# Seven quarter products for the second expert matmul, with paced loads and turns at PSUM banks in the schedule

## The chip, the cores and the metric

The kernel runs on one core of a Trainium2 chip. The metric is the time of one execution in device microseconds. Before the change the median was 1172.03 us of three runs (1170.56 to 1175.1).

Words used throughout: PE is the matmul engine (PEld its weight load), DVE the vector engine, ACT the scalar engine, POOL the GpSimd engine, SP the engine that issues some of the DMA. SBUF is the on-chip memory, PSUM the memory, in banks, that matmuls write into. The granted PE clock is the share of PE's full clock that the chip let it have. To "turn" is to transpose. A "group" is 512 tokens; there are nine groups and eight experts. A "pair" is two attention heads of one batch; there are 32 pairs.

## The reference

```python
def phi(x):                       # attention with exp features
    proj = einsum('bhsd,df->bhsf', x, w_phi)
    proj = proj - max(abs(proj), axis=-1)
    return concatenate([exp(proj), exp(-proj)])
q_p, k_p = phi(q), phi(k)
kv = einsum('bhsf,bhsd->bhfd', k_p, v);  z = sum(k_p, axis=2)
x  = einsum(q_p, kv) / (einsum(q_p, z) + 1e-6)          # -> 4608 x 512
P  = 8 rounds of row and column normalising of exp(x @ w_gate)
for e in range(8):
    h = maximum(x @ w1[e], 0)     # 4608 x 1024
    out += P[:, e] * (h @ w2[e])  # 4608 x 512
```

Batch 8, 8 heads, 576 positions of 64, 128 features; tokens 4608, model width 512, expert width 1024.

## The kernel before

The kernel does not write its instructions in program order. It records every operation with a modelled duration, then a list scheduler (`Plan`) puts them in order of modelled start time, engine by engine. The engines follow that fixed order; each waits, on the chip, for what its next instruction really depends on. So the modelled times decide only the order.

```python
    def start(self, o, free):            # modelled start of an operation
        t = max(free, o.ready)           # engine free, dependencies done
        ...                              # a buffer of the ring is free
        return t
```

Expert 0 is interleaved with attention, one unit per pair with a lag of six pairs, since attention loads DVE and ACT more than PE. Its weights are loaded whole, after the first pair:

```python
    def stage_b(j):
        ...
            if j == 0:
                W[0] = load_w(0, [(xbs[j], 0)])     # two DMAs of 2 MB (f32)
    def stage_a(i):
        ...
            load_qk(b + 1, 2 * pr, 4, t)            # next batch, no gate
            load_v(b + 1, 2 * pr, 4, t)
            if b + 1 >= 1:
                turn_qk(t)                          # DMA transpose for every batch but the first
```

After attention and the routing (P), experts 1 to 7 run, group after group. For each group 32 matmuls of 128x512 make the hidden layer (`up`, ACT does the relu into `hT`), and 32 more the output (`down`), each output tile of 128 tokens being scaled by P and added to `acc` by DVE:

```python
            for t0 in range(0, 4, 1):
                py = down(w2, hT, range(t0, t0 + 1), ["P"])    # 8 matmuls of 128x512
                ...
                    if e == 1:
                        pool(850, ... tensor_scalar(acc *= P[:, :, 0]))
                    dve(560, ... scalar_tensor_tensor(acc += P * py))
```

The softmax here doesn't subtract the row's maximum and nothing guards it: scores larger than these inputs give would overflow.

## Time and profile before

| | before |
|---|---|
| median time | 1172.03 us |
| PE busy | 1120.7 us, 96% |
| DVE, ACT, POOL busy | 35%, 44%, 18% |
| first up-matmul of expert 1 | 295.9 us |
| from there to the end | 874.7 us |
| period of one group of experts 1 to 7 | 13.81 us |

First, the busy time of each engine in four stretches of the kernel before (microseconds from the start of the span, engine by engine with the count of instructions; then the granted PE clock, the share of the DMA engines' time that packets took, which can exceed 1, and GB/s).

```profile
core 0: us, PE busy (x) PEld busy (x) DVE busy (x) ACT busy (x) POOL busy (x), PEclk, DMA share, GB/s
0.00:100.00 100.00, 71.29 (x665) 45.06 (x672) 66.42 (x157) 65.69 (x167) 62.67 (x119) 0.85 1.13 153
100.00:200.00 100.00, 91.99 (x983) 58.28 (x997) 85.89 (x208) 88.07 (x228) 57.85 (x118) 1.00 0.74 123
200.00:300.00 100.00, 95.36 (x784) 53.35 (x796) 70.31 (x168) 58.44 (x136) 40.21 (x62) 0.98 0.23 43
600.00:700.00 100.00, 99.53 (x456) 45.35 (x464) 21.79 (x29) 34.19 (x58) 1.64 (x2) 1.00 0.14 22
```

In the expert stage (last line) PE has hardly a gap and the rest is mostly idle: there only less PE work helps. In the first 250 us PE idles at times; between 100 and 200 us DVE and ACT are 86 and 88% busy. In the first 100 us the granted clock is 0.85; the lowest part is this:

```profile
30.00:50.00 20.00, 12.78 (x120) 8.77 (x119) 10.88 (x29) 6.10 (x19) 6.69 (x17) 0.50 1.40 157
```

The PE timeline of the kernel before, in one group of the expert stage (start, length, operation, count):

```profile
703.39 0.59 PE L353 MATMUL P_7735<-w_6754,hT 128*128 128x512 bf16 x2
703.83 0.81 PE L353 MATMUL P_7739<-xT,w_6625 128*128 128x512 bf16 x3
...
710.73 1.46 PE L353 MATMUL P_7735<-w_6754,hT 128*128 128x512 bf16 x6
712.03 1.89 PE L353 MATMUL P_7794<-w_6754,hT 128*128 128x512 bf16 x8
```

The up-matmuls start at 703.83 and, a period later, again at 717.64: 13.81 us for 64 matmuls, 0.216 us each.

The chain of waits of the kernel before, in its first 60 us, has one piece that stands out, and the copies that end each pair (DVE, xT) show what it did:

```profile
25.62 20.93 DMA w_442<-in_moe_w_dram
46.60 0.61 PE P_738 L353
```

```profile
L581 DVE COPY xT<-P_676 x1: 414/414/414, 43.2 to 43.2; 128x512 bf16<-128x512 bf16 x1
L581 DVE COPY xT<-P_1087 x1: 424/424/424, 74.0 to 74.0; 128x512 bf16<-128x512 bf16 x1
L581 DVE COPY xT<-P_1205 x1: 411/411/411, 80.9 to 80.9; 128x512 bf16<-128x512 bf16 x1
```

PE stood in front of expert 0's first matmul until w1 had landed at 46.6 us (its wait there was 2.5 us by the view of waits); the scores of the fifth pair were behind it in PE's order and started at 60.0 us. Pair 4 was done at 43.2 us, pair 5 at 74.0. The last pair was done at 250.6 us.

In the score step DVE (largest absolute value) and ACT (two exponentials) read the same PSUM bank. The timeline of ACT and DVE there (in brackets: idle time before, and what ended it):

```profile
149.34 0.61 ACT L349 ACTIVATE k_2627<-P_2611 128x512 bf16<-128x512 f32 x1
149.99 0.69 DVE L345 TENSOR_REDUCE m<-P_2611 128x4 f32<-128x512 f32 x1 [0.29 <-ACT k_2627 L349]
150.71 0.60 ACT L349 ACTIVATE k_2638<-P_2611 128x512 bf16<-128x512 f32 x1 [0.76 <-DVE m L345]
```

All three read bank P_2611. DVE waits until ACT's first read is over, and ACT's second read waits 0.76 us for DVE. Nothing but the shared bank connects them.

### The profile page before, as it was taken

The page shows a single profiled execution, that of the slowest core. Times are in us where ns is not written, and L with a number is a line of the kernel's source. Part 1 is how long each engine was busy: PE and PEld are TensorE (multiplying, and loading weights), DVE is VectorE, ACT ScalarE, POOL GpSimd, SP SyncE. Part 2 cuts the span into 40 slices and gives each one's busy share as a digit, 9 for nine tenths or more (in the row PEclk, how much of TensorE's full clock was granted, in tenths as well). Part 3 has the DMA queues.
Part 4 walks back from the last instruction along what each step waited for, and adds up shares of the span by engine and source line. Part 5 has one row for each costly group of instructions (what it writes and reads, how often), then busy time and mean ns, then how long its engine had stood idle before and what let it go on. Part 6 is the DMA issues. An engine that isn't in the chain of part 4 may idle for free.

```text
span 1170.6 us, 15841 instructions
## 1 busy us (share of the span) xinstructions
PE 1120.7 (96%) x6361; PEld 549.3 (47%) x6476; DVE 411.9 (35%) x783; ACT 510.9 (44%) x1028; POOL 208.9 (18%) x333
## 2 busy tenths in 40 slices
PE   5777999999999999999999999999999999999998
PEld 3444656654444444444444444444444444444443
DVE  6478888875122222222222222222222222222222
ACT  6488988843433333333333333333333333333331
POOL 9365555513960000000000000000000000000000
PEclk8699999999999999999999999999999999999999
DMA  9988776600040040003100220022000400002112
GB/s 175 156 136 132 131 116 113 127 1 1 1 71 2 3 70 1 1 1 46 28 1 1 36 36 1 1 37 36 1 1 4 69 1 1 1 1 73 72 72 108
DMA packets 87242, 54.45 MB, mean 47 GB/s; under 512 B 47616, under 2 KB 80512, under 8 KB 87168
## 3 DMA queue, kind: packets, MB, share of 16 engines
q0 software_dynamic: 38448, 26.23, 16.7%
q1 hardware_dynamic: 48720, 27.20, 10.2%
q8 instruction: 50, 0.82, 0.3%
q14 instruction: 24, 0.20, 0.1%
HBM read 61.95 MB, written 9.44 MB: 61 GB/s over the span
## 4 chain that ended last, share of the span: by engine, by line
PE 84%; ACT 6%; DVE 4%; DMA 3%; issue 2%; POOL 1%; ACTq 0%; DVEq 0%; POOLq 0%
DMA w_442<-in_moe_w_dram 2%; DVE m L345 1%; DVE xb L559 1%; DMA qkT<-qk 1%; DMA qk_r<-in_q_dram 1%; ACT hT L631 0%; POOL qk L293 0%; DVE rec L557 0%; PE P_4657 L353 0%; POOL qk_r L336 0%; DVE xb_r L564 0%; DVE m_r L345 0%; PE P_4707 L353 0%; PE P_10337 L353 0%; PE P_9770 L353 0%
## 5 line engine op out<-in xcount | busy, mean ns | idle before, releaser
L353 PEld LDWEIGHTS <-hT 128*128 128x128 bf16 x2304 | 225.1, 98 | 264.8 <-issue 2.2
L353 PEld LDWEIGHTS <-w_3748 128*128 128x128 bf16 x288 | 28.2, 98 | 34.0
L353 PEld LDWEIGHTS <-w_5820 128*128 128x128 bf16 x288 | 28.2, 98 | 34.0
L353 PEld LDWEIGHTS <-w_8235 128*128 128x128 bf16 x288 | 28.2, 98 | 34.0
L353 PEld LDWEIGHTS <-w_9040 128*128 128x128 bf16 x288 | 28.2, 98 | 34.0
L353 PEld LDWEIGHTS <-w_5377 128*128 128x128 bf16 x288 | 28.2, 98 | 33.9
L353 PEld LDWEIGHTS <-w_7430 128*128 128x128 bf16 x288 | 28.2, 98 | 34.0
L353 PEld LDWEIGHTS <-w_6625 128*128 128x128 bf16 x288 | 28.2, 98 | 34.0
L353 PEld LDWEIGHTS <-w_442 128*128 128x128 bf16 x288 | 26.6, 100 | 28.6 <-issue 6.5
L353 PEld LDWEIGHTS <-qkT 128*128 128x128 bf16 x256 | 24.8, 101 | 19.7 <-issue 3.6
L282 POOL DMA_DIRECT2D w_6625<-in_moe_w_dram x1 | 0.8, 754 | 103.1 <-PE P_6616 L353 103.1
L282 POOL DMA_DIRECT2D w_8235<-in_moe_w_dram x1 | 0.8, 752 | 103.1 <-PE P_8226 L353 103.1
L282 POOL DMA_DIRECT2D w_9040<-in_moe_w_dram x1 | 0.8, 752 | 103.1 <-PE P_9031 L353 103.1
L282 POOL DMA_DIRECT2D w_7430<-in_moe_w_dram x1 | 0.8, 752 | 103.1 <-PE P_7421 L353 103.1
L293 POOL DMA_DIRECT2D qk<-in_k_dram x17 | 13.6, 801 | 10.3 <-DMA qkT<-qk 5.6
L293 POOL DMA_DIRECT2D qk<-in_q_dram x17 | 13.0, 762 | 0.0
L850 POOL TENSOR_SCALAR acc_82<-acc_82,P 128x512 f32<-128x512 f32 x4 | 6.2, 1555 | 37.3 <-DVE P L814 37.3
L282 POOL DMA_DIRECT2D w_5820<-in_moe_w_dram x1 | 0.8, 752 | 67.3 <-PE P_5811 L353 67.3
L578 PEld LDWEIGHTS <-xb 128*128 128x128 bf16 x128 | 8.7, 101 | 5.7 <-issue 3.8
L353 PEld LDWEIGHTS <-wphi_72 128*128 128x128 bf16 x72 | 6.7, 102 | 4.9 <-issue 4.0
L349 ACT ACTIVATE r<-m 128x8 f32<-128x8 f32 x32 | 7.7, 239 | 0.0
L854 DVE SCALAR_TENSOR_TENSOR acc_82<-P_5169,P,acc_82 128x512 f32<-128x512 f32 x1 | 0.8, 751 | 16.7 <-PE P_5169 L353 16.7
(3557 smaller groups left out, 2621.8 us busy)
## 6 DMA issues: line engine op xcount, KB each, us to landing
v_m<-in_v_dram SPq DMA_DIRECT2D x15, 512.0 KB, 4.7
qk<-in_k_dram POOLq DMA_DIRECT2D x15, 256.0 KB, 5.2
qk<-in_q_dram POOLq DMA_DIRECT2D x15, 256.0 KB, 5.8
w_442<-in_moe_w_dram POOLq DMA_DIRECT2D x1, 1024.0 KB, 20.9
w_458<-in_moe_w_dram POOLq DMA_DIRECT2D x1, 1024.0 KB, 27.1
w_3748<-in_moe_w_dram POOLq DMA_DIRECT2D x1, 1024.0 KB, 9.4
w_3770<-in_moe_w_dram POOLq DMA_DIRECT2D x1, 1024.0 KB, 15.1
w_5377<-in_moe_w_dram POOLq DMA_DIRECT2D x1, 1024.0 KB, 8.3
```

What stands on the lines that cost most here:

```text
L282: dma("POOL", 2 << 20, 280, lambda: nc.gpsimd.dma_start(out=w1(), in_=moe_w1[e].rearrange("(c p) f -> p c f", p=128)), r, [w1])
L293: dma("POOL", nh << 17, 230, lambda x=x, src=src: nc.gpsimd.dma_start(out=t["qk"]()[:, x, o:o + nh], in_=src[b, hh:hh + nh, 0:SM].rearrang ...
L345: dve(el, lambda: nc.vector.tensor_reduce(out=dst(), in_=src(), axis=AX.X, op=ALU.max, apply_absolute_value=True), r, w)
L349: act(el, lambda: nc.scalar.activation(out=dst(), in_=src(), func=ACT.Exp, bias=0.0, scale=scale), r, w)
L353: nc.tensor.matmul(out_, lhsT=lhsT, rhs=rhs, start=start, stop=stop)
L559: dve(256, lambda: nc.vector.tensor_tensor(out=xb()[:, :, h * 64:h * 64 + 64], in0=num()[:, 0:4, 0:D], in1=rec()[:, 0:4, None].to_broadcas ...
L578: pe(128, lambda j=j: nc.tensor.transpose(bf(pxt)[:, j * 128:j * 128 + 128], xb()[:, j, :], ident), [(xb, 0), (xb, 1), "ident"], [pxt])
L850: pool(850, lambda g=g, ts=ts: nc.gpsimd.tensor_scalar(out=acc[g][:, ts, :], in0=acc[g][:, ts, :], scalar1=P[:, 4 * g + ts, 0:1], scalar2= ...
L854: dve(560, lambda g=g, ts=ts, i=i, py=py, e=e: nc.vector.scalar_tensor_tensor(out=acc[g][:, ts, :], in0=py()[:, 512 * i:512 * i + 512], sc ...
```

## The change

The intent: cut the second expert matmul of experts 1 to 7 into quarters (two halves of the tokens and of the contraction, two halves of the contraction and of the output) and compute it with seven products of quarters in place of eight, with Strassen's scheme in Winograd's form. A product is 8 matmuls of 128x256, so 56 of them replace 32 of 128x512, an eighth less PE work in the second matmul. The sums of quarters of w2 (T) are made once per expert on POOL, those of h (S) once per group, two on DVE and two on POOL. Three PSUM banks serve a group; the bank x holds four products one after the other, each added to what is there, and DVE reads it between. In the same change come a new start (expert 0's weights in eight pieces, loads gated on the progress of the pairs, the second batch turned by PE instead of by DMA) and a rule in the scheduler: an operation on a PSUM bank starts, in the model, only after another engine's last use of that bank has ended ("turns"). The scaling of `acc` by expert 0's P moves from POOL to ACT.

The diff, cut to its core (cuts marked with ...):

```diff
@@ def start(self, o, free)
+            elif b.last is not None and b.last.eng != o.eng:
+                t = max(t, b.last.end)
@@ def schedule(self)
             for b in o.bufs:
+                if b.ring.psum:
+                    b.last = o
...
@@ def rest_a / def pair_a
-        if b < 1:
+        if b < 2:                      # turn by PE
@@ def stage_a(i)
+        gt = [("max", 0, i - 1)] if i >= 1 else []
...
-            load_qk(b + 1, 2 * pr, 4, t)
-            load_v(b + 1, 2 * pr, 4, t)
-            if b + 1 >= 1:
+            load_qk(b + 1, 2 * pr, 4, t, gt)
+            load_v(b + 1, 2 * pr, 4, t, gt)
+            if b + 1 >= 2:
                 turn_qk(t)
...
+        n = i - 2
+        if 0 <= n < 8 * 1 and n % 1 == 0:
...
+                    load_w0(1 * (n // 1) + y, [("max", 0, i - 1)] if i >= 1 else [])
@@ def stage_b(j)
-            if j == 0:
-                W[0] = load_w(0, [(xbs[j], 0)])
@@
+    def sums_w(w2):                    # four POOL subtractions of 128x1024 per expert
...
+    def down7(e, g, hT, w2, T):
...
+        add(pool, 2, lambda: a(0, 0), lambda: a(1, 0), ALU.subtract, hk[0])
+        add(dve, 0, lambda: a(1, 0), lambda: a(1, 1), ALU.add, hk[0] + hk[1])
+        add(dve, 1, lambda: S[0](), lambda: a(0, 0), ALU.subtract, [S[0]] + hk[0])
+        add(pool, 3, lambda: a(0, 1), lambda: S[1](), ALU.subtract, [S[1]] + hk[1])
...
+        product(y, lambda: a(0, 1), lambda: b(1, 0), hk[1], True)
+        read(y, 0, 0)                                  # read: two DVE operations of 128x256
+        product(x, lambda: a(0, 0), lambda: b(0, 0), hk[0], True)
...                                                     # ACT copies x to U, POOL adds U to acc
+        product(z, lambda: S[0](), lambda: T()[:, 0], [S[0], (T, 0)], True)
+        read(z, 1, 1)
+        product(x, lambda: S[1](), lambda: T()[:, 1], [S[1], (T, 1)], False)
+        read(x, 0, 1)
+        product(x, lambda: S[2](), lambda: T()[:, 2], [S[2], (T, 2)], False)
+        read(x, 1, 1)
+        product(z, lambda: S[3](), lambda: b(1, 1), [S[3]], False)
+        read(z, 0, 1)
+        product(x, lambda: a(1, 1), lambda: T()[:, 3], hk[1] + [(T, 3)], False)
+        read(x, 1, 0)
```

More of the change, by code (lines that the diff above doesn't have):

```diff
@@ L21, in __init__ @@
         self.ring, self.t, self.slot, self.left, self.end = ring, None, None, 0, 0.0
+        self.last = None
     def __call__(self):
@@ L29, with __init__ @@
 class Ring:
-    def __init__(self, pool, shape, dtype, tag, bufs):
+    def __init__(self, pool, shape, dtype, tag, bufs, psum=False):
+        self.psum = psum
         self.free = [(0.0, i) for i in range(bufs)]
@@ L201 @@
     P = const.tile([128, NT, E], FP32, name="P")
-    vrd = [[const.tile([128, NP, 2, D1], BF16, name=f"vrd{i}{x}") for x in range(2)]
-           for i in range(2)]
     NA = 5
@@ L209 @@
     a_in = tc.alloc_tile_pool(name="a_in", bufs=1)
+    vrd = [[a_in.tile([128, NP, 2, D1], BF16, name=f"vrd{i}{x}") for x in range(2)]
+           for i in range(2)]
     a_t = tc.alloc_tile_pool(name="a_t", bufs=1)
@@ L236, in ring @@
         R[tag] = Ring((lambda: p) if not isinstance(p, str) else (lambda: late[p]),
-                      shape, dtype, tag, bufs)
+                      shape, dtype, tag, bufs, p is ps)
     ring(wp, [128, 4, FF], BF16, "w1", 2)
@@ L263 @@
         ring(a_s, [128, 8], FP32, f"em{x}", 2)
+    ring("s_p", [128, 4, 4, 256], BF16, "T", 2)
+    ring("s_p", [128, 4, 256], BF16, "S", 8)
+    ring("s_p", [128, 2, 256], FP32, "U", 2)
     ring("s_p", [128, NT, E], FP32, "u", 1)
@@ L282, in load_w, with load_w0, load_qk @@
         dma("POOL", 2 << 20, 280, lambda: nc.gpsimd.dma_start(
-            out=w1(), in_=moe_w1[e].rearrange("(c p) f -> p c f", p=128)), r, [w1])
+            out=w1(), in_=moe_w1[e].rearrange("(c p) f -> p c f", p=128)),
+            r, [(w1, i) for i in range(4)])
         dma("POOL", 2 << 20, 280, lambda: nc.gpsimd.dma_start(
-            out=w2(), in_=moe_w2[e].rearrange("(c p) f -> p c f", p=128)), r, [w2])
+            out=w2(), in_=moe_w2[e].rearrange("(c p) f -> p c f", p=128)),
+            r, [(w2, i) for i in range(4)])
         return w1, w2
-    def load_qk(b, hh, nh, t):
+    def load_w0(i, r):
+        w1, w2 = W[0]
+        n = i % 4
+        if i < 4:
+            dma("POOL", 1 << 19, 250, lambda: nc.gpsimd.dma_start(
+                out=w1()[:, :, n * 256:(n + 1) * 256],
+                in_=moe_w1[0].rearrange("(c p) f -> p c f", p=128)
+                [:, :, n * 256:(n + 1) * 256]), r, [(w1, n)])
+        else:
+            dma("POOL", 1 << 19, 280, lambda: nc.gpsimd.dma_start(
+                out=w2()[:, 2 * n:2 * n + 2, :],
+                in_=moe_w2[0].rearrange("(c p) f -> p c f", p=128)
+                [:, 2 * n:2 * n + 2]), r, [(w2, n)])
+    def load_qk(b, hh, nh, t, r=()):
         o = hh % 4
@@ L295, in load_qk, with load_v @@
                 in_=src[b, hh:hh + nh, 0:SM].rearrange("h (p j) d -> p h (j d)", j=NJ)),
-                w=[(t["qk"], x, i) for i in keys])
-    def load_v(b, hh, nh, t):
+                r, [(t["qk"], x, i) for i in keys])
+    def load_v(b, hh, nh, t, r=()):
         o = hh % 4
@@ L303, in load_v @@
             in_=v[b, hh:hh + nh, 0:SM].rearrange("h (p j) d -> p h (j d)", j=NJ)),
-            w=[(t["v"], i) for i in keys])
+            r, [(t["v"], i) for i in keys])
     def turn_qk(t, pr=None):
@@ L323, in new_half, with load_rests @@
         return {"qk": new("qk"), "T": new("qkT"), "v": new("v_m")}
-    def load_rests(b0, nb):
+    def load_rests(b0, nb, r=()):
         t = {"qk": new("qk_r"), "v": new("v_r"), "b0": b0}
@@ L336, in load_rests @@
                     nc.gpsimd.dma_start(out=t["qk"]()[rows, 0:NP * nb, x, :], in_=part(src)),
-                    w=[(t["qk"], h, x)])
+                    r, [(t["qk"], h, x)])
             dma("SP", nb << 16, 150, lambda rows=rows, part=part: nc.sync.dma_start(
-                out=t["v"]()[rows, 0:NP * nb], in_=part(v)), w=[(t["v"], h)])
+                out=t["v"]()[rows, 0:NP * nb], in_=part(v)), r, [(t["v"], h)])
         for b in range(b0, b0 + nb):
@@ L421, in pair_a @@
         s = {}
-        if b < 1:
+        if b < 2:
             for x in (1, 0):
@@ L457, in scores @@
                       lambda pp=pp: pp().rearrange("p (a b) -> p a b", a=4 * n),
-                      [pp], [(m, x, c0)])
+                      [pp], [(m, x, c0), ("max", x, NP * b + pr)])
                 if x == 1:
@@ L629, in up @@
                         xT[:, dc, g * 512:(g + 1) * 512], dc == 0, dc == NP - 1),
-                        xkeys(g, dc) + [w1, *r], [ph, *w], [hT])
+                        xkeys(g, dc) + [(w1, (f0 + i) // 2), *r], [ph, *w], [hT])
             act(512 * n, lambda f0=f0, ph=ph: nc.scalar.activation(
@@ L642, in down @@
                     w2()[:, fc, :], fc == 0, fc == 7),
-                    [(hT, f) for f in (range(8) if fc == 0 else (fc,))] + [w2, *r], [(py, i)])
+                    [(hT, f) for f in (range(8) if fc == 0 else (fc,))]
+                    + [(w2, f) for f in range(4)] + [*r], [(py, i)])
         return py
@@ L681 @@
     load_v(0, 0, 2, halves[0, 0])
-    if 1 == 0:
+    if 2 == 0:
         turn_qk(halves[0, 0], 0)
@@ L692 @@
     load_v(0, 2, 2, halves[0, 0])
-    if 1 == 0:
+    if 2 == 0:
         turn_qk(halves[0, 0], 1)
@@ L696 @@
     load_v(0, 4, 4, halves[0, 1])
-    if 1 == 0:
+    if 2 == 0:
         turn_qk(halves[0, 1])
@@ L708 @@
     rs, st = {}, {}
+    W[0] = (new("w1"), new("w2"))
     def expert0(i):
@@ L728, in stage_a @@
             t = halves[b + 1, pr // 2]
-            load_qk(b + 1, 2 * pr, 4, t)
-            load_v(b + 1, 2 * pr, 4, t)
-            if b + 1 >= 1:
+            load_qk(b + 1, 2 * pr, 4, t, gt)
+            load_v(b + 1, 2 * pr, 4, t, gt)
+            if b + 1 >= 2:
                 turn_qk(t)
-        if pr == 1 and b in (0, 3, 6):
-            load_rests(b + 1, min(3, B - b - 1))
+        if pr == 1 and b in (0, 1, 4):
+            load_rests(b + 1, 1 if b == 0 else 3, gt)
+        n = i - 2
+        if 0 <= n < 8 * 1 and n % 1 == 0:
+            for y in range(1):
+                if 1 * (n // 1) + y < 8:
+                    load_w0(1 * (n // 1) + y, [("max", 0, i - 1)] if i >= 1 else [])
     NS = 4 * B
@@ L828, in store @@
                     [:, ts - 1:ts + 1], in_=acc[g][:, ts - 1:ts + 1, :]),
-                    [("acc", g, ts - 1), ("acc", g, ts)], [("out", g, ts)])
+                    [("acc", g, t, j) for t in (ts - 1, ts) for j in range(2)], [("out", g, ts)])
         else:
@@ L835, in store, with t @@
                     out=out[b * S + SM:(b + 1) * S], in_=acc[8][rows, ts, :]),
-                    [("acc", 8, ts)], [("out", 8, b)])
+                    [("acc", 8, ts, j) for j in range(2)], [("out", 8, b)])
+    def sums_w(w2):
+        b = {(i, j): (lambda i=i, j=j: w2()[:, 4 * i:4 * i + 4, 256 * j:256 * j + 256])
+             for i in range(2) for j in range(2)}
+        T = new("T")
+        def t(n):
+            return T()[:, n]
+        wk = [(w2, i) for i in range(4)]
+        for n, x, y, r in ((0, b[0, 1], b[0, 0], []), (1, b[1, 1], lambda: t(0), [0]),
+                           (2, b[1, 1], b[0, 1], []), (3, b[1, 0], lambda: t(1), [1])):
+            pool(1024, lambda n=n, x=x, y=y: nc.gpsimd.tensor_tensor(
+                out=t(n), in0=x(), in1=y(), op=ALU.subtract),
+                wk + ["late"] + [(T, i) for i in r], [(T, n)])
+        return T
@@ new lines, in down7, with a, b, add @@
+    def down7(e, g, hT, w2, T):
+        def a(i, j):
+            return hT()[:, 4 * j:4 * j + 4, 256 * i:256 * i + 256]
+        def b(i, j):
+            return w2()[:, 4 * i:4 * i + 4, 256 * j:256 * j + 256]
+        S = [new("S") for _ in range(4)]
+        hk = [[(hT, f) for f in range(4 * j, 4 * j + 4)] for j in range(2)]
+        wk = [(w2, i) for i in range(4)]
+        def add(eng, n, x, y, op, r):
+            f = nc.vector if eng is dve else nc.gpsimd
+            eng(512 if eng is dve else 1024,
+                lambda: f.tensor_tensor(out=S[n](), in0=x(), in1=y(), op=op), r, [S[n]])
+        add(pool, 2, lambda: a(0, 0), lambda: a(1, 0), ALU.subtract, hk[0])
+        add(dve, 0, lambda: a(1, 0), lambda: a(1, 1), ALU.add, hk[0] + hk[1])
+        add(dve, 1, lambda: S[0](), lambda: a(0, 0), ALU.subtract, [S[0]] + hk[0])
+        add(pool, 3, lambda: a(0, 1), lambda: S[1](), ALU.subtract, [S[1]] + hk[1])
+        def product(bank, lhs, rhs, r, first):
+            for i in range(2):
+                for k in range(4):
+                    z = i == 0 and k == 0
+                    pe(256, lambda i=i, k=k, z=z: nc.tensor.matmul(
+                        bank()[:, 256 * i:256 * i + 256], lhsT=lhs()[:, k, 128 * i:128 * i + 128],
+                        rhs=rhs()[:, k, :], start=first and z, stop=k == 3,
+                        skip_group_check=True), r + wk + (["P"] if z else []), [bank])
+        def read(bank, i, j):
+            for n in range(2):
+                ts = 2 * i + n
+                dve(350, lambda n=n, ts=ts: nc.vector.scalar_tensor_tensor(
+                    out=acc[g][:, ts, 256 * j:256 * j + 256],
+                    in0=bank()[:, 256 * n:256 * n + 256], scalar=P[:, 4 * g + ts, e:e + 1],
+                    in1=acc[g][:, ts, 256 * j:256 * j + 256], op0=ALU.mult, op1=ALU.add),
+                    [bank, "P"], [("acc", g, ts, j)])
+        if e == 1:
+            for ts in range(4):
+                act(512, lambda ts=ts: nc.scalar.activation(
+                    out=acc[g][:, ts, :], in_=acc[g][:, ts, :], func=ACT.Copy, bias=0.0,
+                    scale=P[:, 4 * g + ts, 0:1]), ["P", ("acc", g, ts)],
+                    [("acc", g, ts, j) for j in range(2)])
+        x, y, z = new("P1"), new("P1"), new("P1")
+        product(y, lambda: a(0, 1), lambda: b(1, 0), hk[1], True)
+        read(y, 0, 0)
+        product(x, lambda: a(0, 0), lambda: b(0, 0), hk[0], True)
+        u = new("U")
+        for n in range(2):
+            act(256, lambda n=n: nc.scalar.activation(
+                out=u()[:, n, :], in_=x()[:, 256 * n:256 * n + 256], func=ACT.Copy, bias=0.0,
+                scale=P[:, 4 * g + n, e:e + 1]), [x, "P"], [(u, n)])
+        pool(512, lambda: nc.gpsimd.tensor_tensor(
+            out=acc[g][:, 0:2, 0:256], in0=acc[g][:, 0:2, 0:256], in1=u(), op=ALU.add),
+            [(u, 0), (u, 1)], [("acc", g, n, 0) for n in range(2)])
+        product(z, lambda: S[0](), lambda: T()[:, 0], [S[0], (T, 0)], True)
[8 more added lines that the diff above has]
+        read(x, 1, 0)
@@ L838 @@
     for e in range(1, E):
         w1, w2 = load_w(e, [("xT", 5, 3)])
+        T = sums_w(w2)
         for g in (list(range(NG)) if e < E - 1 else [8] + list(range(8))):
@@ L842 @@
             up(w1, g, hT, range(8), 1, r=["up0"])
-            for t0 in range(0, 4, 1):
-                plan.prio = 100
-                py = down(w2, hT, range(t0, t0 + 1), ["P"])
-                plan.prio = 0
-                for i in range(1):
-                    ts = t0 + i
-                    if e == 1:
-                        pool(850, lambda g=g, ts=ts: nc.gpsimd.tensor_scalar(
-                            out=acc[g][:, ts, :], in0=acc[g][:, ts, :],
-                            scalar1=P[:, 4 * g + ts, 0:1], scalar2=None, op0=ALU.mult),
-                            ["P"], [("acc", g, ts)])
-                    dve(560, lambda g=g, ts=ts, i=i, py=py, e=e: nc.vector.scalar_tensor_tensor(
-                        out=acc[g][:, ts, :], in0=py()[:, 512 * i:512 * i + 512],
-                        scalar=P[:, 4 * g + ts, e:e + 1],
-                        in1=acc[g][:, ts, :], op0=ALU.mult, op1=ALU.add),
-                        [(py, i), "P"], [("acc", g, ts)])
-                    if e == E - 1:
-                        store(g, ts)
+            plan.prio = 100
+            down7(e, g, hT, w2, T)
+            plan.prio = 0
+            if e == E - 1:
+                for ts in range(4):
+                    store(g, ts)
     plan.run(tc)
```

## The prediction

> **What bounds it now.** PE: busy 1120.7 of 1170.6 us (busy table), 84% of the chain of waits. From 300 us on it is 99.5% busy (busy by stretch) at clock 1.00. The timeline repeats every 13.81 us per token group: 32 + 32 matmuls of 128x512, 0.216 us each. The other engines idle there (per 100 us: DVE 21, ACT 35, POOL 1).
>
> The first 250 us are attention with some of expert 0. PE is 71% busy in 0-100 us at clock 0.85, then 92 and 95%. The chain holds one DMA of 20.9 us there (expert 0's w1, 25.6 to 46.5 us). Expert 0's matmuls come ahead of the fifth head pair, whose scores start only at 60.0 us. The xT copies show pair 4 at 43.2, pair 5 at 74.0 us, later pairs every 6.5 us.
>
> **The change, steady state.** 32 matmuls of 512 columns become 56 of 256. Two of 256 take 0.38 us in the trace, one 0.27, so one costs 0.109; eight of 65 columns with fresh weights take 0.26 us, so a weight load per matmul does not bind. 56 x 0.109 = 6.1 against 6.9 us: a group should fall from 13.8 to 13.0 us, over 63 groups -51 us.
>
> Added per group:
> - DVE: twelve 256-column reads instead of four 512-column ones (0.75 us each, so about 0.49 each by estimate; 5.8 us), and two bf16 sums of 1024. The Trainium skill (VectorE: DVE Perf Modes) lets a bf16 tensor_tensor produce two elements a cycle; the trace agrees for copies (512 bf16 in 0.41 us against 0.68 for an f32 reduce of 512), so about 0.65 us each. Together 7 of 13 us.
> - ACT: two scaled copies, about 0.4 us each; 5.6 us in all. The 36 scalings by P leave POOL (1.55 us) for ACT.
> - POOL: two sums of 1024 and an f32 add, about 5 us (512 took 1.04); four T sums per expert.
>
> One bank takes four products in turn, with two DVE reads (0.9-1.0 us) between. In the order of instructions at least 14 matmuls (1.5 us) of other banks stand between. Counting through a burst, PE's margin at the tightest point (last product in the bank) is about 0.2 us: mostly no wait. The skill (SBUF — State Buffer, Who interferes with whom) says a DVE instruction with two SBUF inputs contends with GpSimd reads; I expect a few collisions while T sums run. I charge 5 us of waits in all, and 2 us for the last group.
>
> **The change, first stage.** Paced weight pieces, PE transposes for batch 1 (36, about 2 us PE) instead of slow queue transposes, bank turns in the schedule. The gap between pairs 4 and 5 should shrink from 31 to under 12 us. Expert 0's matmuls done in the gap must fit elsewhere: about 204 us of PE work at 90% puts the end of attention near 236 instead of 252 us. About -15 us.
>
> **Sum.** 1172 - 51 + 5 + 2 - 15 = 1113 us. Range 1097 to 1133. Faster by over 2%: 0.95; within: 0.04; slower: 0.01.
>
> **Right or wrong is shown by.** Group period 13.0 us; 256-column matmuls 0.109 us apart; PE over 98% busy after 300 us; DVE about 55%, ACT 45%, POOL 38% busy; no long w1 DMA in the chain; last xT copy near 236 us.
>
> **What would make it wrong.** 256-column matmuls further apart; bf16 sums at one element a cycle (+0.5 us each), which eat the 0.2 us margin and cost 0.5 us a group (30 us); POOL slower than 2 us a sum or locking out DVE; DMA-bound start.

## More of the kernel before

The profiled executions are single ones; their spans are about 2 us shorter than the times (1.7 to 2.5).

## The result, and the profile after

The changed kernel is correct and takes 1111.61 us, median of three runs (1110.51 to 1114.47). The ratio to the kernel before is 0.9485, 95% interval 0.9444 to 0.9526. A ratio is always the mean time of one kernel's runs over that of the other's of the same rounds, so it is not quite the ratio of the medians quoted.

| | before | after | difference |
|---|---|---|---|
| first up-matmul of expert 1 | 295.9 us | 272.8 us | -23.1 |
| from there to the end of the span | 874.7 us | 835.7 us | -39.0 |
| group period | 13.81 us | 13.02 us | -0.79 |
| last pair of attention done | 250.6 us | 226.6 us | -24.0 |

The same stretches as above, of the changed kernel:

```profile
core 0: us, PE busy (x) PEld busy (x) DVE busy (x) ACT busy (x) POOL busy (x), PEclk, DMA share, GB/s
0.00:100.00 100.00, 79.85 (x874) 50.04 (x875) 83.39 (x204) 81.17 (x210) 75.42 (x146) 1.00 1.05 152
100.00:200.00 100.00, 99.10 (x1081) 63.59 (x1079) 89.58 (x219) 91.08 (x239) 60.27 (x118) 1.00 0.92 146
200.00:300.00 100.00, 94.54 (x680) 52.05 (x677) 64.61 (x137) 65.18 (x135) 41.47 (x43) 0.97 0.18 30
600.00:700.00 100.00, 99.04 (x658) 64.03 (x656) 47.69 (x102) 43.65 (x78) 53.95 (x30) 1.00 0.13 22
```

PE is still the limit of the expert stage, with DVE, ACT and POOL now about half busy. Between 100 and 200 us PE went from 92 to 99%: attention no longer leaves PE gaps. In the first 100 us the granted clock is 1.00 instead of 0.85, and in the stretch where it was 0.50 before:

```profile
30.00:50.00 20.00, 15.91 (x207) 10.26 (x206) 16.56 (x42) 15.71 (x43) 16.52 (x32) 1.00 0.97 137
```

I had noted the clock of 0.85 and given it no term. PE's busy time in the first 100 us, weighted with the share of the clock that was missing (an estimate from the clock records of the traces), is 11 us in the kernel before and 0 in this one; in e1 it is 4, in e5 5, in e6 7, and in e7, e9 and e10 about 9 us. So part of what the start gains may be PE at its full clock. Whether the clock fell because PE had gaps, or the gaps grew because it fell, no run here separates.

The PE timeline of the changed kernel, around one burst of products:

```profile
699.91 0.27 PE L915 MATMUL P_9341<-T,S 128*128 128x256 bf16 x1
700.02 1.04 PE L915 MATMUL P_9299<-T,S 128*128 128x256 bf16 x8
...
702.42 1.04 PE L915 MATMUL P_9299<-T,S 128*128 128x256 bf16 x8
...
704.83 1.04 PE L915 MATMUL P_9299<-T,hT 128*128 128x256 bf16 x8
705.70 0.49 PE L915 MATMUL P_9473<-T,S 128*128 128x256 bf16 x3
706.03 1.03 PE L379 MATMUL P_9498<-xT,w_7425 128*128 128x512 bf16 x4
```

Eight matmuls of 128x256 take 0.87 us to the start of the next line, 0.109 us each, with a fresh weight load for each one. From the up-matmuls at 706.03 to those of the next group at 719.05 it is 13.02 us. P_9299 is the shared bank, used at 700.02, 702.42 and 704.83; between, PE works for other banks. In DVE's timeline the two reads of the second of these products begin at 703.50 and are over at 704.38, 0.45 us before PE comes back to the bank.

The pairs of the changed kernel (there is no long weight DMA in the first 60 us of its chain of waits any more, so that line has no counterpart):

```profile
L607 DVE COPY xT<-P_868 x1: 413/413/413, 45.3 to 45.3; 128x512 bf16<-128x512 bf16 x1
L607 DVE COPY xT<-P_1029 x1: 410/410/410, 55.9 to 55.9; 128x512 bf16<-128x512 bf16 x1
L607 DVE COPY xT<-P_1108 x1: 412/412/412, 58.0 to 58.0; 128x512 bf16<-128x512 bf16 x1
```

The gap between pairs 4 and 5 shrank from 30.8 to 10.6 us.

One group period per expert is not 13.02 but 13.83 to 14.17 us, five times in all, each time with a PE wait for DVE. This is one of the places, POOL and DVE of the changed kernel in order of time:

```profile
661.48 2.12 POOL L882 TENSOR_TENSOR T<-w_8851 128x1024 bf16<-128x1024 bf16 x1
663.55 2.58 POOL L882 TENSOR_TENSOR T<-w_8851,T 128x1024 bf16<-128x1024 bf16 x1
```

```profile
661.68 2.47 DVE L904 TENSOR_TENSOR S<-hT 128x1024 bf16<-128x1024 bf16 x1
664.07 0.86 DVE L924 SCALAR_TENSOR_TENSOR acc_79<-P_8942,P,acc_79 128x256 f32<-128x256 f32 x2
```

The DVE sum began 0.2 us after the POOL sum and took 2.47 us instead of its usual 0.68: it ended 0.55 us after POOL's first sum did. The next POOL sum then took 2.58 instead of 2.12. The Trainium skill (SBUF — State Buffer, section Who interferes with whom) says that a DVE instruction with two SBUF inputs contends with GpSimd reads and that whoever issues first keeps the other out for the whole instruction. These lines agree with it, and experiment e3 tests it.

### The profile page after: what moved, and what is told of

It is laid out like the page before. It is cut to its first block, busy times and chain, and to the rows that moved or that the text cites. A ratio compares the mean times of both kernels' runs of the same rounds, so it can differ in the third digit from the quotient of the medians.

```text
span 1108.5 us, 20141 instructions
## 1 busy us (share of the span) xinstructions
PE 1072.2 (97%) x8024; PEld 693.4 (63%) x8024; DVE 637.6 (58%) x1422; ACT 579.9 (52%) x1190; POOL 565.1 (51%) x520
## 4 chain that ended last, share of the span: by engine, by line
PE 86%; ACT 5%; DVE 4%; issue 1%; POOL 0%; DVEq 0%; ACTq 0%
DVE acc_79 L924 1%; ACT hT L657 1%; DVE S L904 1%; PE P_5334 L915 0%; PE P_13295 L915 0%; PE P_13027 L915 0%; PE P_10496 L915 0%; PE P_9961 L915 0%; PE P_7970 L915 0%; PE P_6773 L915 0%; PE P_6238 L915 0%; PE P_12759 L915 0%; PE P_12625 L915 0%; PE P_12353 L915 0%; PE P_12221 L915 0%
## 5 line engine op out<-in xcount | busy, mean ns | idle before, releaser
L904 POOL TENSOR_TENSOR S<-hT,S 128x1024 bf16<-128x1024 bf16 x63 | 133.9, 2125 | 284.8 <-DVE S L904 284.8
L915 PEld LDWEIGHTS <-S 128*128 128x128 bf16 x2016 | 197.5, 98 | 38.3 <-issue 1.4
L904 POOL TENSOR_TENSOR S<-hT 128x1024 bf16<-128x1024 bf16 x63 | 133.5, 2118 | 102.2 <-ACT hT L657 102.2
L915 PEld LDWEIGHTS <-hT 128*128 128x128 bf16 x1512 | 148.1, 98 | 25.2 <-issue 5.6
L904 DVE TENSOR_TENSOR S<-hT 128x1024 bf16<-128x1024 bf16 x63 | 51.9, 824 | 14.0 <-ACT hT L657 14.0
L379 PEld LDWEIGHTS <-w_3836 128*128 128x128 bf16 x288 | 28.2, 98 | 32.3
L379 PEld LDWEIGHTS <-w_11016 128*128 128x128 bf16 x288 | 28.2, 98 | 32.0
L379 PEld LDWEIGHTS <-w_7425 128*128 128x128 bf16 x288 | 28.2, 98 | 32.1
L379 PEld LDWEIGHTS <-w_6228 128*128 128x128 bf16 x288 | 28.2, 98 | 32.1
L379 PEld LDWEIGHTS <-w_9819 128*128 128x128 bf16 x288 | 28.2, 98 | 32.1
L379 PEld LDWEIGHTS <-w_8622 128*128 128x128 bf16 x288 | 28.1, 98 | 32.1
L379 PEld LDWEIGHTS <-w_5074 128*128 128x128 bf16 x288 | 28.1, 98 | 32.1
L904 DVE TENSOR_TENSOR S<-S,hT 128x1024 bf16<-128x1024 bf16 x63 | 47.6, 756 | 0.0
L379 PEld LDWEIGHTS <-hT 128*128 128x128 bf16 x288 | 28.1, 101 | 26.3 <-issue 2.3
L379 PEld LDWEIGHTS <-w_429 128*128 128x128 bf16 x288 | 25.8, 98 | 23.5 <-issue 2.1
L291 POOL DMA_DIRECT2D w_5074<-in_moe_w_dram x1 | 0.8, 823 | 29.0 <-PE P_5064 L379 29.0
L945 POOL TENSOR_TENSOR acc_78<-acc_78,U 128x512 f32<-128x512 f32 x7 | 9.3, 1330 | 0.0
L452 PEld LDWEIGHTS <-qk 128*128 128x128 bf16 x64 | 4.5, 102 | 7.5 <-DMA qk<-in_k_dram 4.9
## 6 DMA issues: line engine op xcount, KB each, us to landing
w_3836<-in_moe_w_dram POOLq DMA_DIRECT2D x1, 1024.0 KB, 10.7
```

The source lines that it names most:

```text
L291: dma("POOL", 2 << 20, 280, lambda: nc.gpsimd.dma_start(out=w1(), in_=moe_w1[e].rearrange("(c p) f -> p c f", p=128)), r, [(w1, i) for i i ...
L379: nc.tensor.matmul(out_, lhsT=lhsT, rhs=rhs, start=start, stop=stop)
L452: pe(128, lambda x=x, c=c, ptr=ptr: nc.tensor.transpose(bf(ptr)[:, c * 128:(c + 1) * 128], t["qk"]()[:, x, h0 + c // 2, (c % 2) * 128:(c % ...
L904: lambda: f.tensor_tensor(out=S[n](), in0=x(), in1=y(), op=op), r, [S[n]])
L915: pe(256, lambda i=i, k=k, z=z: nc.tensor.matmul(bank()[:, 256 * i:256 * i + 256], lhsT=lhs()[:, k, 128 * i:128 * i + 128], rhs=rhs()[:, k ...
L945: pool(512, lambda: nc.gpsimd.tensor_tensor(out=acc[g][:, 0:2, 0:256], in0=acc[g][:, 0:2, 0:256], in1=u(), op=ALU.add), [(u, 0), (u, 1)], ...
```

## The experiments

Twelve kernels ran, all correct. "Changed" is the changed kernel. Ratios are to the kernel before, from rounds on the same chip; there were three such batches (e1 to e4, e5 to e8, e9 to e12), in which the kernel before took 1172.48, 1171.65 and 1171.02 us.

| run | what | median us | ratio, 95% |
|---|---|---|---|
| (changed) | all parts | 1111.61 | 0.9485 (0.9444 to 0.9526) |
| e1 | products alone | 1137.05 | 0.9699 (0.9679 to 0.9719) |
| e2 | first stage alone | 1150.34 | 0.9812 (0.9796 to 0.9829) |
| e3 | T sums on DVE | 1105.1 | 0.9427 (0.9411 to 0.9442) |
| e4 | last group plain | 1110.8 | 0.9473 (0.9457 to 0.949) |
| e5 | without paced loads | 1118.93 | 0.9536 (0.9517 to 0.9555) |
| e6 | batch 1 turned by DMA | 1119.26 | 0.9557 (0.9528 to 0.9586) |
| e7 | without turns | 1155.76 | 0.9857 (0.9837 to 0.9877) |
| e8 | small extra DVE work | 1115.58 | 0.9517 (0.9502 to 0.9531) |
| e9 | products and turns only | 1128.21 | 0.962 (0.9587 to 0.9653) |
| e10 | products and PE turning only | 1153.51 | 0.9846 (0.9831 to 0.9861) |
| e11 | large extra DVE work | 1139.01 | 0.9714 (0.9694 to 0.9735) |
| e12 | e3 and e4 together | 1104.73 | 0.9429 (0.9415 to 0.9443) |

My theory was that two separate gains add up, one from the products and one from the start. The rival was that the products need the new schedule to pay.

### e1: the products alone

The changed kernel with the scheduler's rule, the gates, the pieces and batch 1's PE transposes taken back. PE's order of instructions is that of the kernel before through the whole first stage.

```diff
-            elif b.last is not None and b.last.eng != o.eng:
-                t = max(t, b.last.end)
-        if b < 2:
+        if b < 1:
-        gt = [("max", 0, i - 1)] if i >= 1 else []
+        gt = []
...
+            if j == 0:
+                W[0] = load_w(0, [(xbs[j], 0)])
```

> The products of seven alone, on the loads, transposes and schedule of the kernel before (same order of instructions on PE through the whole first stage). My theory is that the gain is a sum of two separate parts, read from the two traces: from expert 1's first up-matmul to the end 874.7 us before and 835.7 after (39.0 less), and up to that matmul 295.9 before and 272.8 after (23.1 less). Then this runs in about 1172 - 39 = 1133 us (1130 to 1137), its first up-matmul of expert 1 stays at 295 to 297 us. The rival, that the products only pay on the new start (for example because T sums or the first groups would be late without it), expects over 1142 us.

Measured: 1137.05 us (1134.65 to 1138.7). The first up-matmul of expert 1 came at 301.0 us, and from there to the end of the span it took 835.9 us, against 835.7 in the changed kernel. So the products are worth 38.8 us wherever the stage begins, and the theory holds for them. The time missed the expected band by a hair, because the start took 5 us longer than in the profile of before with the same order on PE and DVE (pair 5 at 76.2 instead of 74.0 us, last pair at 254.9 instead of 250.6). About 2 us of this are w1, which took 22.8 us to land instead of 20.9 and came at 49.1 instead of 46.6 us. What made the rest was not found; the runs of one kernel spread over 4 us (e1: 1134.65 to 1138.7).

### e2: the first stage alone

The changed kernel with the old second matmul.

```diff
-            down7(e, g, hT, w2, T)
+            for t0 in range(0, 4, 1):
+                py = down(w2, hT, range(t0, t0 + 1), ["P"])
...
```

> The new first stage (paced loads, PE transposes for batch 1, bank turns) with the second matmul as before, 32 of 512 columns. Separate parts: about 1172 - 23 = 1149 us (1145 to 1153), expert 1's first up-matmul at 271 to 275 us, group period 13.8 us. My prediction on record had -15 for this part, that is 1157. The rival (bank turns matter in the expert stage, too) expects the stretch after 273 us to differ from the 874.7 us of before by more than 3 us.

Measured: 1150.34 us; the first up-matmul of expert 1 at 274.4 us, 874.9 us from there to the end of the span of 1149.3, group period 13.81 us. As the sum of parts expects: 1172.5 - 1137.05 and 1172.5 - 1150.34 make 57.6 us together, and the change as a whole gains 60.4. The missing 2.8 us are less than the 5 us by which e1's start was late in its profile.

### e3: the T sums on DVE

```diff
-            pool(1024, lambda n=n, x=x, y=y: nc.gpsimd.tensor_tensor(
+            dve(512, lambda n=n, x=x, y=y: nc.vector.tensor_tensor(
                 out=t(n), in0=x(), in1=y(), op=ALU.subtract),
```

> The four T sums per expert go from POOL to DVE (0.68 us each there by the trace, 2.12 on POOL), where DVE idles 6.5 us a group. Once per expert the group period is 13.85 instead of 13.02 us, and there one DVE sum took 2.47 instead of 0.68 us while POOL was in a T sum. If it is that DVE and POOL block each other for a whole instruction, all group periods become 13.02, no DVE sum is over 0.75 us in the steady state, and 6 x 0.83 = 5 us and up to 2 more at expert 1's start go away: ratio to the changed kernel 0.994, about 1105 us. If the wait comes from w2's landing or from PE order, the time stays within 1 us of 1111.

Measured: 1105.1 us (1103.73 to 1105.93), and every steady group period was 13.02 us. The DVE sums of the changed kernel and of e3 (count, then shortest, median and longest in ns):

```profile
L904 DVE TENSOR_TENSOR S<-hT x63: 678/681/2468, 283.0 to 1094.1; 128x1024 bf16<-128x1024 bf16 x63
L904 DVE TENSOR_TENSOR S<-S,hT x63: 678/681/2499, 283.7 to 1096.5; 128x1024 bf16<-128x1024 bf16 x63
```

```profile
L904 DVE TENSOR_TENSOR S<-hT x63: 678/681/691, 282.5 to 1087.7; 128x1024 bf16<-128x1024 bf16 x63
L904 DVE TENSOR_TENSOR S<-S,hT x63: 678/681/693, 283.2 to 1090.1; 128x1024 bf16<-128x1024 bf16 x63
```

With the T sums off POOL no S sum on DVE takes over 0.7 us. But the sign that I had named, no DVE sum over 0.75 us, was missed by the T sums, which are now DVE's own:

```profile
L882 DVE TENSOR_TENSOR T<-w x14: 685/1130/2611, 229.2 to 885.2; 128x1024 bf16<-128x1024 bf16 x14
L882 DVE TENSOR_TENSOR T<-w,T x14: 678/688/2608, 230.4 to 887.6; 128x1024 bf16<-128x1024 bf16 x14
```

In the steady state two of the four per expert take 1.13 and 1.75 us, each of them while POOL runs one of its own sums. So the two engines still lock each other out; the edit did not end the lock, it moved it to where DVE's lateness does not reach PE. Landing of w2 and PE order were not the cause of the long periods. About 4.5 us came from the five long periods; expert 1's first two groups, from their first up-matmul to that of the third group, took 25.7 instead of 27.6 us.

### e4: the last group plain

```diff
+            if e == E - 1 and g == 7:
+                for ts in range(4):
+                    py = down(w2, hT, range(ts, ts + 1), ["P"])
...
+            else:
+                down7(e, g, hT, w2, T)
```

> The last group of the last expert takes 32 matmuls of 512 columns in place of the seven products. In the changed kernel PE waits there 0.44 + 0.97 us for DVE reads in the turns at one bank, with nothing else to do, and DVE starts its last read 1.12 us later. Plain costs 6.9 against 6.1 us of PE work and saves about 1.5 to 2.5 us of waits: -0.7 to -1.7 us, about 1110 us. A tail bound by the last store alone expects no change.

Measured: 1110.8 us, ratio 0.9473 against 0.9485. The intervals overlap, so the times alone do not resolve it. In the traces, from the start of the last up-matmuls to the end of the span it takes 21.9 us against 23.2 in the changed kernel, which is the expected size.

### e5: without paced loads

```diff
-        gt = [("max", 0, i - 1)] if i >= 1 else []
+        gt = []
...
+            if j == 0:
+                W[0] = load_w(0, [(xbs[j], 0)])
```

> The changed kernel with the loads of before: no gates on q, k, v and rest loads, and expert 0's weights as two whole loads after the first head pair, not in eight paced pieces. Before, w1 took 20.9 us to land and PE stood in front of expert 0's first matmul until 46.6 us, with the fifth pair's scores behind it. If that is most of the 23 us, this loses 12 to 20 us: 1124 to 1132, pair 5's xT copy at 65 us or later instead of 55.9. If the PE transposes are what freed the start, it loses under 5 us.

Measured: 1118.93 us, 7.3 us more than the changed kernel. Neither expectation was right. Pair 5 came at 59.1 us, hardly later than the 55.9 of the changed kernel, so there was no gap between pairs 4 and 5; the lateness sits on both sides of it. Pair 4 itself was done at 52.4 instead of 45.3 us, with a PE wait of 4.4 us for POOL before it, and pair 9 at 95.0 instead of 80.5 us. (The profiled run is the slowest of its five, 1123.05 us.)

### e6: batch 1 turned by DMA again

```diff
-        if b < 2:
+        if b < 1:
-            if b + 1 >= 2:
+            if b + 1 >= 1:
                 turn_qk(t)
```

> The changed kernel with batch 1 turned by queue transposes as before, the rest kept. In the trace of before, the first two queue transposes of batch 1 took 6.2 and 12.9 us on a busy DMA, against 2.0 us median. If they hold up pairs 4 to 7, this loses 5 to 12 us: 1116 to 1124, gap between pairs 4 and 5 over 15 us instead of 10.6. If pacing alone frees the DMA, the transposes are fast too and it loses under 3 us.

Measured: 1119.26 us, 7.7 us more, inside the first expectation; but the gap between pairs 4 and 5 was 10.7 us, as in the changed kernel, not over 15. The time went before and after: pair 4 at 51.1 instead of 45.3, last pair at 233.2 instead of 226.6 us. The chain of waits of e6 in its first 60 us shows what came before pair 4:

```profile
23.21 10.41 DMA qkT<-qk
```

One queue transpose took 10.41 us to land, against a median of 5.9 us in the kernel before, and PE waited 3.4 us for it. So slow queue transposes do cost time, at another place than I expected. The granted clock was also lower here, 0.86 in the first 50 us against 1.00, and how the 7.7 us divide between the two is open.

### e7: without turns in the schedule

```diff
-            elif b.last is not None and b.last.eng != o.eng:
-                t = max(t, b.last.end)
```

> The changed kernel, the schedule made without the rule of turns at a PSUM bank (the waits themselves stay, only the order of instructions changes). In the expert stage the order differs little, and the group period should stay at 13.02 us. In attention I expect the order to fit the real waits worse: 3 to 8 us slower, 1115 to 1120, spread over pairs 5 to 28 rather than in one gap. The rival, that turns matter for the seven products in one bank, expects group periods over 13.1 us.

Measured: 1155.76 us, 44 us more. I had expected 3 to 8. The rival was wrong as well: the steady group periods stayed at 13.02 us. All of it is attention: from pair 9 to pair 32 it took 173.7 us, against 146.1 in the changed kernel and 152.3 in the kernel before (27.6 us more than the changed kernel; the other 17 us came before pair 9). This is what ACT waited for there, between 110 and 220 us of e7 (line waited for, us in total, times, longest):

```profile
ACT k L373 <- DVE m L369: 16.7, 26, 0.8
ACT q L373 <- PE P L563: 5.0, 5, 2.1
```

Adding up the same view for DVE and for the other kernels, in the same window: ACT waited for DVE, and DVE for ACT, over a bank of scores:

| | ACT for DVE | DVE for ACT | pairs 9 to 32 |
|---|---|---|---|
| before | 11.1 us, 17 times | 3.6 us, 7 times | 152.3 us |
| changed | 0 | 0 | 146.1 us |
| e7, without turns | 17.5 us, 27 times | 12.2 us, 18 times | 173.7 us |

Between 30 and 100 us it is the same in e7: ACT waited 12.9 us (18 times) for DVE, DVE 10.9 us (15 times) for ACT; in the changed kernel neither did.

It is the ping-pong at one bank shown in the profile of before. The scheduler without the rule does not know that two engines cannot read one bank together, so it puts DVE and ACT at the same bank at the same modelled time, and on the chip they alternate with both standing still in turn. With the rule it orders them so that each works at another bank meanwhile. The Trainium skill (PSUM — Partial Sum Buffer, section PSUM bank collisions raise a hardware error) says that two engines must be kept off one bank, two readers included, by semaphores; the waits of 0.76 us in the trace are such waits.

### e8 and e11: how much slack the shared bank has

One extra DVE reduction of 16x8 (e8), or two of 36x8 (e11), with an unused result, ahead of the reads of the third product in the shared bank. The modelled time is unchanged and so is PE's order of instructions.

```diff
-                dve(350, lambda n=n, ts=ts: nc.vector.scalar_tensor_tensor(
+                dve(350, lambda n=n, ts=ts: [nc.vector.tensor_reduce(
+                    out=scr[:, 0:16], in_=L[:, 0:16, :], axis=AX.X, op=ALU.add)
+                    for _ in range(1 if filler and n == 0 else 0)
+                    ] + [nc.vector.scalar_tensor_tensor(
```

> The same order of instructions, with one extra DVE reduction of 16x8 f32 (unused result, about 0.2 us) ahead of the read of the third product in the shared bank, in every one of the 63 groups. My prediction counted PE's margin there as about 0.2 us; in the changed kernel's trace DVE's read ends about 0.4 us before PE takes the bank again. So: no change, within 1 us of the changed kernel, group period 13.02 us. If the chain through the bank has no slack, the cost is 63 x 0.2 = 13 us.

Measured for e8: 1115.58 us. The group period stayed at 13.02 us, so the slack in a group is over 0.2 us. The 4 us that it took more are elsewhere: its start was 2.0 us later (first up-matmul of expert 1 at 274.8 us; other runs with the same start lie between 272.7 and 275.4), and the long period of each expert grew, to 14.14 to 14.57 us, together 1.8 us. So the band of 1 us for the time was missed, the expectation for the period met.

> As the small extra DVE reduction, but two of 36x8 f32 per group (0.45 us each by the trace of before, about 0.75 to 0.9 us together). The small one (0.2 us) left all group periods but the one per expert at 13.02 us, so the slack is over 0.2 us; the trace of the changed kernel shows 0.45 us from the end of DVE's read to PE's next use of the bank. With 0.4 us of slack each group grows by 0.35 to 0.5 us: period 13.4 to 13.5 us, 22 to 32 us in all, 1134 to 1144. If DVE's work were hidden by other slack, no change.

Measured for e11: 1139.01 us, inside the band, and a group period of 13.38 us, a hair under it. DVE and PE of e11 in one group:

```profile
719.57 0.93 DVE L925 TENSOR_REDUCE scr<-L 128x36 f32<-128x288 f32 x2
720.42 0.87 DVE L928 SCALAR_TENSOR_TENSOR acc<-P,P,acc 128x256 f32<-128x256 f32 x2
```

```profile
721.34 1.03 PE L916 MATMUL P<-T,hT 128*128 128x256 bf16 x8 [0.20 <-DVE acc L928]
```

The extra work holds DVE for 0.85 us (719.57 to 720.42), the group grew by 13.38 - 13.02 = 0.36 us, so the slack of the shared bank was about 0.49 us a group, if beyond it each us of DVE's lateness costs PE one us. That this agrees with the 0.45 us read from the trace supports it; a second size of extra work beyond the slack was not run.

### e9 and e10: which parts belong together

e9 is e1 plus the rule of turns; e10 is e7 without the gates and pieces, so of the first stage only the PE transposes for batch 1 are left, and the new order in which the small rest loads are batched, which e5 keeps too.

```diff
# e9, against e1
+            elif b.last is not None and b.last.eng != o.eng:
+                t = max(t, b.last.end)
# e10, against e7
-        gt = [("max", 0, i - 1)] if i >= 1 else []
+        gt = []
+            if j == 0:
+                W[0] = load_w(0, [(xbs[j], 0)])
```

> The seven products with the rule of turns in the schedule, but loads and batch 1's queue transposes as before: the products-alone kernel (1137 us) plus turns. Without turns the changed kernel lost 44 us, more than the whole first stage had gained, so the parts of the first stage are not independent. If the rule by itself is the larger part of the gain, this runs in 1115 to 1125 us, head pairs 9 to 32 at 6.4 us or less each against 6.6 before. If the rule is only needed to repair what the gates on the loads do to the order, it stays at 1133 to 1140 us.

Measured for e9: 1128.21 us (1121.44 to 1130.38, a wide spread), between the two expectations. The old gap is back (pair 4 at 41.8, pair 5 at 76.6 us), but pairs 9 to 32 took 145.0 us against 154.4 in e1, and in the window of 110 to 220 us neither DVE nor ACT waited for the other at all. The rule alone is worth about 9 us in both the time and the pairs 9 to 32; it does nothing for the gap.

> The changed kernel without gates and paced pieces and without the rule of turns; only batch 1's PE transposes are left of the first stage. Tells which of the two made the run without turns so slow (1156 against 1137 for the old first stage). If the gates on the loads did, this is near 1137 us or a little better (1130 to 1140); if the PE transposes did, it is near 1156 (1148 to 1160).

Measured for e10: 1153.51 us. It is the PE transposes, not the gates, that cost so much without the rule: ACT waited 28 times (18.6 us) for DVE and DVE 20 times (13.6 us) for ACT in the same window, pairs 9 to 32 took 168.1 us. Why turning only batch 1 on PE (with the new batching of the rest loads) makes the order of all later pairs worse stays open. The scheduler's order follows its modelled times, and an earlier start shifts them all; I did not trace which shift does it.

All seven combinations that ran, with the products in each (median us); the eighth, paced loads alone, did not run. "PE turning" includes the batching of the rest loads, except in e6, which keeps the batching and gives up the turning alone:

| turns | paced loads | PE turning | us |
|---|---|---|---|
| no | no | no | 1137.05 (e1) |
| yes | no | no | 1128.21 (e9) |
| no | no | yes | 1153.51 (e10) |
| no | yes | yes | 1155.76 (e7) |
| yes | yes | no | 1119.26 (e6) |
| yes | no | yes | 1118.93 (e5) |
| yes | yes | yes | 1111.61 (changed) |

With turns, each of the other two is worth 7 to 9 us, whether the other is there or not. Without turns, PE turning costs 16 us and pacing, on top of it, gains nothing. So the parts of the first stage do not add up without the rule, while the first stage and the products do add up.

### e12: a version that beats both

e3 and e4 together, that is, both edits above.

> T sums on DVE and the last group plain, the two changes that helped alone (ratios to the kernel before 0.9427 and 0.9473, against 0.9485 for the changed kernel): 1104 us (1102 to 1106), ratio 0.942, every group period 13.02 us.

Measured: 1104.73 us (1104.48 to 1105.03), ratio 0.9429. Every steady period was 13.02 us. It beats the kernel before and the changed kernel, but not e3 (0.9427) by anything these rounds resolve. From the start of the last up-matmuls to the end it takes 22.1 us against 23.0 in e3, so about a microsecond is gained at the end; in the profiled runs e12's start was 2.4 us later than e3's.

## Why the prediction was right

The predicted time was 1113 us, the measured one 1111.61 us. The mechanisms held, but two terms of the sum were mis-sized in opposite directions.

- "56 x 0.109 = 6.1 against 6.9 us: a group should fall from 13.8 to 13.0 us": the period is 13.02 us and eight matmuls take 0.87 us. Right. 63 x (13.81 - 13.02) is 49.8 us, and I had -51.
- "about 0.49 each by estimate" for the short reads: two of them take 0.88 us, about 0.48 us each in the records. "about 0.65 us each" for the bf16 sums: 0.68 us. The skill's statement in VectorE: DVE Perf Modes, section The perf-mode tier table, that a bf16 tensor_tensor makes two elements a cycle, agrees: at one element a cycle of the 0.96 GHz that the page's specifications give, 1024 would take 1.07 us by estimate.
- "PE's margin at the tightest point ... is about 0.2 us: mostly no wait": no wait in a plain group, right. The margin is 0.45 us in the trace and 0.49 us by e11. I had added up single durations; back to back, DVE operations overlap a little.
- "I charge 5 us of waits in all, and 2 us for the last group": this term was too small. The stage from expert 1 on gained 39.0 us, 10.8 less than 49.8. Five long periods cost 4.5 us together. Expert 1's first two groups took 27.6 us to the third group's first up-matmul, where their 64 matmuls of 512 columns and 86 of 256 make about 23.2: 4.4 us lost. PE waited there twice for ACT (1.42 and 0.53 us), which was 100% busy from 260 to 290 us (it now scales `acc` and still has the relus); three S sums on DVE took 1.8 to 2.5 us beside POOL's T sums; and the granted clock was 0.83 from 290 to 300 us. About 1.9 us are left for the end and the rest; e4 gained 1.3 at the end. The collisions came where I had put them, while T sums run; what I had not counted was the start of expert 1.
- "The gap between pairs 4 and 5 should shrink from 31 to under 12 us": 10.6 us. Right. I had named the paced loads and the PE transposes together; beside the rule of turns either of them alone closes this gap (e6, e5), and with neither (e9) it is back.
- "about 204 us of PE work at 90% puts the end of attention near 236 instead of 252 us. About -15 us": the end came at 226.6 us and the stage gained 23.1. The work and the rate were both about right: PE was busy 202.8 us up to that point, 89.5% of the time (99.1% between 100 and 200 us made up for the beginning). But 204 us at 90% is 227 us, which is where the end came, and not 236. So the 8 us by which this term was too small are the step from my own two numbers to the end of the stage. I had named "bank turns in the schedule" and given them no term. With the loads and transposes of the change they are worth 44 us (e7), alone about 9 (e9). They took all waits between DVE and ACT over a shared bank out of the middle of attention, which in the kernel before were 24 in 110 us. The clock, 0.85 before and 1.00 after in the first 100 us, had no term either.
- Of the signs that I had named, DVE was 58% busy (55 named), but ACT 52% (45) and POOL 51% (38). PE was 99.5% busy after 300 us all the same (over 98% named).

The start gained 8 us more than predicted and the experts 5 us less, and the two nearly cancelled. The closeness of 1113 to 1111.61 is partly luck.

## What to carry to other kernels

When a stage is bound by PE with DVE, ACT and POOL idle, an eighth of a matmul's work can be bought off with element-wise sums on the idle engines, if the reads of a shared PSUM bank stay inside the time that PE spends at other banks; measure that slack by adding work until PE waits. A scheduler's model has to know each wait that the program really makes: leaving out that two readers of a bank take turns cost 44 us here with the other changes in, and 9 without them, against 7 for the loads. And bulk sums with two SBUF inputs on POOL beside the same on DVE lock each other for whole instructions, so a long one belongs where the lateness does not reach the engine that bounds the stage, as e3 found.

## What the Trainium skill lacked or had wrong

- TensorE: Matmul & The Clock Gate, section Back-to-back issue gap, gives a sustained 131 ns per matmul of 512 columns for a stream of weight loads and matmuls, and says that the isolated N/2.4 + 2.5 ns over-counts there. Here such a stream ran at 216 ns for 512 columns and 109 ns for 256 (N/2.4 + 2.5 gives 215.8 and 109.2), a fresh weight load for each. For these two sizes the formula that the page calls isolated fits, and the sustained figure does not.
- The same page, section LDWEIGHTS, gives P/1.2 ns, 107 ns for 128 columns. The records show about 98 ns, and with 65-column matmuls a weight load and a matmul followed each other every 33 ns (eight in 0.26 us), so the records of successive loads overlap and the formula is not the rate at which loads can follow each other. The section does not say that.
- SBUF — State Buffer, section Who interferes with whom, has the lock between DVE and GpSimd right, but no size for two sums side by side: a bf16 sum of 128x1024 took 2.12 us on POOL and 0.68 us on DVE, and 2.47 us on DVE when it came 0.2 us after POOL's.
- PSUM — Partial Sum Buffer tells that two readers must be kept off one bank, not what it costs when the order is made without it: in e7 27 waits of ACT in 110 us, of at most 0.8 us and 17.5 us together, and 44 us of the whole time. No page has it.
